# Attention's keys transposed and swapped two slots earlier, and the read-back of results two slots later

## The chip, the cores and the metric

The kernel runs on one core of a Trainium2 chip. The metric is the device time of one execution in microseconds (us). The engines are TensorE (PE), VectorE (DVE), ScalarE (ACT) and GpSimd (POOL); SyncE (SP) issues nearly all DMA transfers of this kernel, in one queue and in the order of the program.

## The reference

Only the first of three stages is touched: attention over 4 batches of 8 heads, 576 positions, 64 columns per head, in float32, with rotated queries and keys.

```python
q_rot, k_rot = (rotate(q), rotate(k))     # x1*cos - x2*sin, x1*sin + x2*cos
scores = scale * np.matmul(q_rot, k_rot.transpose(0, 1, 3, 2))
attn = np.exp(scores - np.max(scores, axis=-1, keepdims=True))
attn = attn / (np.sum(attn, axis=-1, keepdims=True) + 1e-09)
return np.matmul(attn, v)
```

Its result, as a matrix x of 2304 tokens by 512 columns, goes through a gated feed-forward layer (`_moe_ref`) and then through a layer of eight experts, each token to one (`_moe2_ref`).

## The kernel before

**Slots and pairs.** Heads are worked on in 16 pairs, numbered 0 to 15. A pair has nine units of 128 rows of queries, and unit u's scores are made in slot u, so that pair p starts at slot 9p, its base. Slots run from -18 to 152. `step(s)` emits the work of a slot in the order of the string ORDER: exp of the unit before (`soft`), scores, matmuls with the values (`pva`, `pvb`), the copy of their results (`pv_out`), transposes of queries or keys (`qk_T`), the maximum, transposes of the exponentials (`trans`), and `jobs`. No scheduler changes it: each engine takes its instructions in program order.

**Preparation of a pair.** The table AT says how many slots from its base each job of a pair stands. The rotated keys (`rope_a`, `rope_u`, `rope_b` on POOL) are split in a rounded part (`rope_h`, DVE) and a rest (`rope_l`, POOL), both held in the tile `natk`. `qk_T` transposes them on PE in three groups of three, each into the one PSUM bank M of the slot, from which ACT copies them to `Ak`. M and the slot's other uses of it share one tile. `swap` copies `Ak` to `Bk` with its two halves of 64 partitions exchanged, by two DMA transfers, and the scores matmuls read both. Queries go the same way, 10 slots ahead, into `Aq` (tiles `rtq`, `ruq`, `natq`). `Ak` and `Bk` have two buffers each, `rawk` and `rawq` one each, so that the load of the next pair's `rawq` waits for `rope_u` of this pair's queries.

**Results.** A pair's output leaves ACT as two tiles x and goes to the DRAM tensor `xT`, one store (L337) for each of its two heads; the reciprocals of the row sums go to `rT` (L359). For the first two chunks of 384 tokens, eight parts in all, the results are read back while attention still runs: `x_load` (L560, and two or four L569 for the reciprocals) at slot X_FROM + 9i for i from 0 to 7, `x_sum` on POOL three slots later, `x_split` on ACT and DVE seven slots later.

**SP's queue.** Nothing on SP is bound to a slot: a transfer is issued when those before it are and when its own waits are over. Besides its data, each transfer waits for the one eight places before it in the queue.

Of the kernel before, what the change touches and what calls it, by code (L numbers as in the profile page):

```python
# [22 lines left out]
class Attention:  # L23
# [6 lines left out]
    def __init__(self, ctx, tc, q, k, v, tabs, xT, rT, ident):  # L30
# [36 lines left out]
        for p in range(self.NPAIR):  # L67
# [1 line left out]

    AT = {"load k": -22, "load q": -18, "load_v": 1, "rope_a k": -18, "rope_u k": -17, "rope_b k": -16, "rope_h k": -12, "rope_l k": -12, "qk k": (-9, -8, -6),
          "swap": -6, "rope_a q": -10, "rope_u q": -10, "rope_b q": -10, "rope_h q": -8, "rope_l q": -7, "qk q": (-5, -3, -2), "q_pad": 1, "v_split": 5}


    AT_FIRST = ({"rope_a k": -18, "rope_a q": -18, "rope_u k": -17, "rope_b k": -16, "rope_h k": -15, "rope_l k": -15, "qk k": (-14, -13, -12), "rope_u q": -16, "rope_b q": -15, "rope_h q": -14, "rope_l q": -14, "swap": -12, "qk q": (-11, -11, -9), "load_v": -13, "q_pad": 2, "v_split": 6, "load k": -18, "load q": -18},
                {"rope_a k": -18, "rope_u k": -18, "rope_b k": -15, "rope_a q": -16, "rope_u q": -16, "rope_b q": -15, "rope_h k": -10, "rope_l k": -9, "rope_h q": -7, "rope_l q": -4, "qk k": (-6, -5, -3), "swap": -1, "qk q": (-3, -2, 0), "q_pad": 1, "load k": -18, "load q": -18, "v_split": 3, "load_v": -1},
                {"rope_a k": -16, "rope_u k": -16, "rope_b k": -13, "rope_h k": -12, "rope_l k": -10, "load k": -17, "load q": -17, "v_split": 5, "rope_l q": -8, "qk k": (-8, -8, -6), "rope_b q": -8, "rope_a q": -8, "q_pad": 0, "rope_u q": -10})

    def plan(self, p):  # L80
        base = p * self.UNITS
        for what, at in (self.AT | dict(enumerate(self.AT_FIRST)).get(p, {})).items():
            name, *n = what.split()
# [1333 lines left out]
def build(tc, ctx, q, k, v, w_gate, w_val, w_out, w_skip, w_route, w1, w2, cos, sin, tok, cf, out):  # L1417
# [14 lines left out]
    with ExitStack() as part:  # L1432
        at = Attention(part, tc, q, k, v, {"c": cos, "s": sin}, xT, rT, ident)
        for s in at.slots():
# [9 lines left out]
            for lag, fn in ((0, m1.x_load), (X_LAG[0], m1.x_sum), (X_LAG[1], m1.x_split)):  # L1444
                i, rest = divmod(s - lag - X_FROM, at.UNITS)
                if rest == 0 and 0 <= i < 2 * KT:
# [16 lines left out]
EARLY = 4  # L1463
SPLIT_FROM = 6
SPLIT_SLOTS = (3, 7)
X_FROM = 55
X_LAG = (3, 7)

# [26 lines left out]
```

## Time and profile before

| what | value |
|---|---|
| median of 3 runs | 1065.49 us (1062.41 to 1065.62) |
| the profiled execution's own time | 1068.54 us |
| its span, first to last instruction | 1066.7 us |
| PE busy | 984.9 us, 92% |
| ACT, DVE and POOL busy from 0 to 328 us | 247.76, 237.78 and 220.01 us |
| scores matmuls of attention | 14 to 328 us |

The span is the time between the first and the last instruction in the trace; 1.9 us lie around it. Attention takes the first 328 us, and the two other stages follow it.

### The profile page before, as it was taken

What the parts mean: (1) busy time and instruction counts of PE and PEld (TensorE: products, weight loads), DVE (VectorE), ACT (ScalarE), POOL (GpSimd) and SP (SyncE); (2) the same over time, 40 slices, a digit from 0 to 9 for tenths busy, and PEclk for the clock granted to TensorE, in tenths of its full rate; (3) what the DMA queues carried; (4) which work ended last, traced back from release to release, by engine and by line L of the source; (5) the groups of instructions that cost most, each with busy time, mean ns of one, the idle gap of its engine ahead of it and who ended that gap; (6) DMA issues with size and microseconds to landing.
All of it is one profiled execution on the core that took longest, in us unless ns stands there. A gap on an engine that the chain in (4) does not pass through costs nothing. (4 is left out here: it accounts for less than half of the span.)

```text
span 1066.7 us, 16446 instructions
## 1 busy us (share of the span) xinstructions
PE 984.9 (92%) x5893; PEld 816.7 (77%) x5893; DVE 559.4 (52%) x962; ACT 479.5 (45%) x1041; POOL 442.6 (41%) x441
## 2 busy tenths in 40 slices
PE   5999998898899889999999999999999948999896
PEld 4687776676677778789999998999999736786643
DVE  6777777676766888873553342332353314315111
ACT  4888878686776333332441322322344104224122
POOL 6586778677711454553125224124153121112111
PEclk8999999899989999999999999999999968999998
DMA  5345455554423433323320310310421469306191
GB/s 172 88 133 128 131 152 144 147 143 123 127 74 131 122 109 113 104 72 88 100 67 8 95 48 8 96 45 8 133 86 41 135 174 356 103 31 211 30 356 61
DMA packets 81276, 119.80 MB, mean 112 GB/s; under 512 B 36469, under 2 KB 47365, under 8 KB 81168
## 3 DMA queue, kind: packets, MB, share of 16 engines
q1 hardware_dynamic: 77712, 110.01, 34.6%
q0 software_dynamic: 3456, 8.45, 2.6%
q8 instruction: 55, 0.90, 0.4%
q14 instruction: 53, 0.43, 0.1%
HBM read 87.73 MB, written 22.75 MB: 104 GB/s over the span
## 5 line engine op out<-in xcount | busy, mean ns | idle before, releaser
L614 POOL TENSOR_TENSOR hl<-h,hh 128x384 fp32r<-128x384 f32 x72 | 77.9, 1081 | 244.1 <-ACT hh L613 237.9
L251 DVE TENSOR_REDUCE nm<-S 128x1 f32<-128x576 f32 x144 | 108.5, 755 | 46.6 <-PE S L239 45.0
L259 ACT ACTIVATE P<-S,nm 128x576 f32<-128x576 f32 x144 | 107.2, 744 | 4.1 <-DVE nm L251 4.0
L613 ACT CAST hh<-h 128x384 fp32r<-128x384 f32 x72 | 37.0, 514 | 142.7 <-DVE h L612 142.7
L611 DVE TENSOR_TENSOR h<-g,h 128x384 f32<-128x384 f32 x72 | 40.0, 556 | 111.8 <-ACT h L610 111.8
L269 PE MATMUL T<-ident,P 128*128 128x128 f32 x576 | 92.3, 285 | 0.0
L239 PE MATMUL S<-Bk,Aq 128*128 128x288 f32 x256 | 75.6, 309 | 16.2 <-DMA Bk<-Ak 16.2
L627 PE MATMUL Y<-ohi,hl 128*128 128x512 f32 x216 | 85.9, 398 | 1.6 <-POOL hl L614 1.6
L627 PE MATMUL Y<-ohi,hh 128*128 128x512 f32 x216 | 87.1, 403 | 0.0
L318 PE MATMUL pv<-pt,rawv 128*64 128x384 f32 (+1 forms) x512 | 84.8, 433 | 1.5 <-ACT pt L284 1.4
L627 PE MATMUL Y<-olo,hh 128*128 128x512 f32 x216 | 85.3, 395 | 0.0
L239 PE MATMUL S<-Ak,Aq 128*128 128x288 f32 x256 | 83.7, 340 | 1.6 <-ACT P L259 1.6
L604 PE MATMUL g<-xa,ghi 128*128 128x384 f32 x216 | 75.5, 350 | 9.2 <-DVE h L611 8.6
L610 ACT ACTIVATE h<-g 128x384 f32<-128x384 f32 x72 | 35.1, 487 | 87.7 <-PE g L606 83.8
L606 PE MATMUL g<-xa,glo 128*128 128x384 f32 x216 | 72.4, 335 | 0.0
L606 PE MATMUL v<-xa,vlo 128*128 128x384 f32 x216 | 72.2, 334 | 0.0
L604 PE MATMUL v<-xa,vhi 128*128 128x384 f32 x216 | 72.1, 334 | 0.0
L269 PEld LDWEIGHTS T<-ident,P 128*128 128x128 f32 x576 | 65.5, 145 | 2.1 <-issue 1.2
L239 PEld LDWEIGHTS S<-Bk,Aq 128*128 128x128 f32 x256 | 51.5, 201 | 18.5 <-issue 18.1
L612 DVE TENSOR_TENSOR h<-v,h 128x384 f32<-128x384 f32 x72 | 40.2, 558 | 47.7 <-PE v L606 45.3
L239 PEld LDWEIGHTS S<-Ak,Aq 128*128 128x128 f32 x256 | 51.1, 200 | 6.3 <-issue 4.2
L282 DVE COPY pt<-T 128x512 f32<-128x512 f32 x64 | 44.2, 690 | 21.8 <-PE T L269 20.3
(267 smaller groups left out, 2543.6 us busy)
## 6 DMA issues: line engine op xcount, KB each, us to landing
wr_s<-in_moe_w_dram SPq DMA_DIRECT2D x46, 512.0 KB
xT<-x SPq DMA_DIRECT2D x32, 288.0 KB
x<-xT SPq DMA_DIRECT2D x24, 384.0 KB
Bk<-Ak SPq DMA_DIRECT2D x30, 288.0 KB
raw<-in_moe_w_gate_dram SPq DMA_DIRECT2D x12, 512.0 KB
raw<-in_moe_w_val_dram SPq DMA_DIRECT2D x12, 512.0 KB
raw<-in_moe_w_out_dram SPq DMA_DIRECT2D x12, 512.0 KB
wr<-in_moe_w_dram SPq DMA_DIRECT2D x10, 512.0 KB
```

Of the source, the lines that this page charges most:

```text
L239: nc.tensor.matmul(ps[:, c, :288], l, r[:, c * 288:(c + 1) * 288], start=(j == 0), stop=(j == len(ops) - 1))
L251: nc.vector.tensor_reduce(nm, st_u["S"], axis=AX.XY, op=ALU.max, negate=True)
L259: nc.scalar.activation(pt.rearrange("p (a b) -> p a b", a=2), st_u["S"], AF.Exp, bias=st_u["nm"], scale=1.0, accum_out=self.pairs[p]["l"][ ...
L269: nc.tensor.transpose(ps[:, kt * P:(kt + 1) * P], pt[:, kt * P:(kt + 1) * P], self.ident)
L282: self.nc.vector.tensor_copy(self.pt[:, :, cols], self.units[u]["T"])
L318: nc.tensor.matmul(ps[a * D:a * D + D, :n], st["raw"]["v"][:, h, 2 * third + a], self.pt[:, 2 * third + a, c0:c0 + n], start=(third == 0), ...
L604: nc.tensor.matmul(ps[m], wh[:, kt, cols], xh, start=(kt == 0), stop=False)
L606: nc.tensor.matmul(ps[m], wl[:, kt, cols], xh, start=False, stop=(kt == KT - 1))
L611: nc.vector.tensor_tensor(h, ps["g"], h, op=ALU.mult)
L612: nc.vector.tensor_tensor(h, ps["v"], h, op=ALU.mult)
L614: nc.gpsimd.tensor_tensor(hl, h, f32(hh), op=ALU.subtract)
L627: nc.tensor.matmul(self.acc[c][t], a[:, cols], b, start=(f == 0 and i == 0), stop=(f == FT - 1 and i == 2))
```

## The change

Three numbers differ. The three groups of a pair's keys are transposed 11, 9 and 8 slots ahead of its base instead of 9, 8 and 6, and `swap` stands 8 slots ahead instead of 6. Pairs 0 and 1 have values of their own for both and stay as they are. Pair 2 has its own for the transposes and now gets the old one for `swap` too, so that pairs 3 to 15 move. X_FROM is 57 instead of 55, which moves all eight `x_load`, `x_sum` and `x_split` by two slots.

```diff
-    AT = {..., "qk k": (-9, -8, -6),
-          "swap": -6, ...}
+    AT = {..., "qk k": (-11, -9, -8),
+          "swap": -8, ...}
...
-                {..., "qk k": (-8, -8, -6), ..., "rope_u q": -10})
+                {..., "qk k": (-8, -8, -6), ..., "rope_u q": -10, "swap": -6})
...
-X_FROM = 55
+X_FROM = 57
```

**SP's queue**, from the read-back of slot 73 (before) on: `x` and `r` are the read-back, `xT` and `rT` the stores of pair 7, `Bk_9` the swap of pair 9, `rawq_11` the queries of pair 11, `raw_11` weights. Before:

```order
L560 DMA x_0_2_2400<-xT_62 128x2x384
L569 DMA r_0_2_2402<-rT_63 64x384 x2
L337 DMA xT_62<-x_7_0_2338 2x64x576
L359 DMA rT_63<-rr_7_2420 9x128
L206 DMA Bk_9_2462<-Ak_9_2340 64x1152
L207 DMA Bk_9_2462<-Ak_9_2340 64x1152
L104 DMA rawk_11_2521<-in_k_dram 128x576
L337 DMA xT_62<-x_7_1_2448 2x64x576
L457 DMA raw_11_2575<-in_moe_w_val_dram 128x1024
L104 DMA rawq_11_2639<-in_q_dram 128x576
```

Of the change, the same stretch, which like the one before follows the six loads of `rawv_8`:

```order
L206 DMA Bk_9_2390<-Ak_9_2281 64x1152
L207 DMA Bk_9_2390<-Ak_9_2281 64x1152
L337 DMA xT_62<-x_7_0_2335 2x64x576
L359 DMA rT_63<-rr_7_2416 9x128
L560 DMA x_0_2_2457<-xT_62 128x2x384
L569 DMA r_0_2_2459<-rT_63 64x384 x2
L104 DMA rawk_11_2512<-in_k_dram 128x576
L337 DMA xT_62<-x_7_1_2444 2x64x576
L457 DMA raw_11_2573<-in_moe_w_val_dram 128x1024
L104 DMA rawq_11_2634<-in_q_dram 128x576
```

Swap and read-back have changed places: the swap now stands ahead of the store of the first head, and the read-back behind it.

**POOL's queue**, around the sums of the same read-back (`natk_10`, `rtq_10` and `ruq_10` are keys and queries of pair 10, `vt_8` values of pair 8). Before:

```order
L576 TENSOR_TENSOR x_0_2_2400<-x_0_2_2400 128x384
L577 TENSOR_TENSOR x_0_2_2400<-x_0_2_2400,r_0_2_2402 128x384
L221 CAST vt_8_2518<-rawv_8_2385 128x2x64
L222 TENSOR_TENSOR vt_8_2518<-rawv_8_2385,vt_8_2518 128x2x64
L164 TENSOR_TENSOR natk_10_2547<-rtk_10_2356,natk_10_2547 128x9x64
L139 TENSOR_TENSOR rtq_10_2606<-rawq_10_2354,c_115 128x576
L147 TENSOR_TENSOR ruq_10_2608<-rawq_10_2354,s_116 128x9x32 x2
L151 TENSOR_TENSOR rtq_10_2606<-rtq_10_2606,ruq_10_2608 128x576
```

Of the change:

```order
L221 CAST vt_8_2509<-rawv_8_2381 128x2x64
L222 TENSOR_TENSOR vt_8_2509<-rawv_8_2381,vt_8_2509 128x2x64
L164 TENSOR_TENSOR natk_10_2538<-rtk_10_2352,natk_10_2538 128x9x64
L576 TENSOR_TENSOR x_0_2_2457<-x_0_2_2457 128x384
L577 TENSOR_TENSOR x_0_2_2457<-x_0_2_2457,r_0_2_2459 128x384
L139 TENSOR_TENSOR rtq_10_2604<-rawq_10_2350,c_115 128x576
L147 TENSOR_TENSOR ruq_10_2606<-rawq_10_2350,s_116 128x9x32 x2
L151 TENSOR_TENSOR rtq_10_2604<-rtq_10_2604,ruq_10_2606 128x576
```

The two sums of the read-back now stand behind the last step of the keys and directly ahead of the queries.

**PE's queue** in slot 70, the eighth of pair 7 (`S_70` and `S_71` are scores, `M_70` the slot's bank, `T_66` transposed exponentials). Before:

```order
L239 MATMUL S_70_2275<-Bk_7_1901,Aq_7_1922 128x288
L177 MATMUL M_70_2282<-identr_110,natq_8_2118 128x128 x3
L269 MATMUL T_66_2289<-ident_66,P_66_2191 128x128 x4
L239 MATMUL S_71_2298<-Ak_7_1779,Aq_7_1922 128x288
L239 MATMUL S_71_2298<-Bk_7_1901,Aq_7_1922 128x288
```

Of the change:

```order
L239 MATMUL S_70_2269<-Bk_7_1833,Aq_7_1917 128x288
L177 MATMUL M_70_2276<-identr_110,natq_8_2116 128x128 x3
L177 MATMUL M_70_2276<-identr_110,natk_9_2261 128x128 x3
L269 MATMUL T_66_2288<-ident_66,P_66_2185 128x128 x4
L239 MATMUL S_71_2297<-Ak_7_1724,Aq_7_1917 128x288
L239 MATMUL S_71_2297<-Bk_7_1833,Aq_7_1917 128x288
```

Slot 9p + 7 now holds two groups of transposes into one bank, the last one of queries and the first one of the next but one pair's keys.

## Rows read from the trace of the kernel before

**Rows 1.** The page's group of scores matmuls that read Bk; idle before, releaser.

```profile
L239 PE MATMUL S<-Bk,Aq 128*128 128x288 f32 x256 | 75.6, 309 | 16.2 <-DMA Bk<-Ak 16.2
```

**Rows 2.** Busy time by stretch: length, PE, PEld, DVE, ACT, POOL, PEclk, DMA, GB/s.

```profile
53.46:125.75 72.29, 72.29 (x562) 56.08 (x562) 56.84 (x89) 61.30 (x152) 53.75 (x59) 1.00 0.50 131
125.75:143.85 18.10, 18.10 (x142) 14.04 (x141) 14.27 (x23) 15.96 (x39) 16.18 (x18) 1.00 0.55 146
143.85:314.07 170.22, 154.56 (x1121) 118.81 (x1121) 119.14 (x184) 126.04 (x313) 114.52 (x125) 0.94 0.48 130
```

**Rows 3.** Timeline of SP, two rounds and a half: start, length, line, transfer.

```profile
126.07 0.33 SPq L104 DMA_DIRECT2D rawq<-in_q_dram  x1
...
130.31 0.61 SPq L118 DMA_DIRECT2D rawv<-in_v_dram  x1
132.24 0.39 SPq L560 DMA_DIRECT2D x<-xT  x1
...
134.36 0.56 SPq L337 DMA_DIRECT2D xT<-x  x1
...
135.54 0.52 SPq L206 DMA_DIRECT2D Bk<-Ak  x1
136.12 0.59 SPq L207 DMA_DIRECT2D Bk<-Ak  x1
...
194.44 0.38 SPq L560 DMA_DIRECT2D x<-xT  x1
...
201.50 0.54 SPq L337 DMA_DIRECT2D xT<-x  x1
205.68 0.38 SPq L104 DMA_DIRECT2D rawq<-in_q_dram  x1
...
214.29 0.38 SPq L560 DMA_DIRECT2D x<-xT  x1
```

**Rows 4.** SP's own waits to 700 us: total, times, longest.

```profile
SPq L560 <- DMA xT<-x: 10.5, 5, 2.6
```

**Rows 5.** SP's timeline near 318 us; then DMA of 322.8:326.2: packets, MB, share.

```profile
318.12 0.54 SPq L337 DMA_DIRECT2D xT<-x  x1
...
q1 hardware_dynamic: 76, 0.18, 13.0%
```

**Rows 6.** DMA queue of SP in 221:226, then in 226.1:227.8: packets, MB, share.

```profile
q1 hardware_dynamic: 359, 0.98, 80.0%
...
q1 hardware_dynamic: 34, 0.10, 21.9%
```

**Rows 7.** Timeline of POOL: read-back sums and the queries of pair 10.

```profile
198.07 1.01 POOL L576 TENSOR_TENSOR x<-x 128x384 f32<-128x384 f32 x1 [4.34 <-DMA x<-xT]
199.15 1.01 POOL L577 TENSOR_TENSOR x<-x,r 128x384 f32<-128x384 f32 x1
...
202.28 1.87 POOL L139 TENSOR_TENSOR rtq<-rawq,c 128x576 f32<-128x576 f32 x1
204.11 1.54 POOL L147 TENSOR_TENSOR ruq<-rawq,s 128x288 f32<-128x288 f32 x2
205.73 1.59 POOL L151 TENSOR_TENSOR rtq<-rtq,ruq 128x576 f32<-128x576 f32 x1
```

**Rows 8.** Timelines of DVE and PE in the second and fourth slot of pair 6.

```profile
129.11 0.69 DVE L158 CAST natq<-rtq 128x576 fp32r<-128x576 f32 x1
129.72 0.68 DVE L282 COPY pt<-T 128x512 f32<-128x512 f32 x1
...
132.44 0.62 PE L269 MATMUL T<-ident,P 128*128 128x128 f32 x4
```

**Rows 9.** Timelines of PE, ACT and POOL in slot 61, the eighth of pair 6.

```profile
139.80 0.37 PE L177 MATMUL M<-identr,natq 128*128 128x128 f32 x3
...
140.31 0.52 ACT L184 ACTIVATE Aq<-M 128x384 fp32r<-128x384 f32 x1
...
139.35 1.43 POOL L164 TENSOR_TENSOR natk<-rtk,natk 128x576 fp32r<-128x576 f32 x1 [0.40 <-PE T L269]
```

More of the change, by code (lines that the diff above doesn't have):

```diff
@@ L68, in __init__ @@
             self.plan(p)
-    AT = {"load k": -22, "load q": -18, "load_v": 1, "rope_a k": -18, "rope_u k": -17, "rope_b k": -16, "rope_h k": -12, "rope_l k": -12, "qk k": (-9, -8, -6),
-          "swap": -6, "rope_a q": -10, "rope_u q": -10, "rope_b q": -10, "rope_h q": -8, "rope_l q": -7, "qk q": (-5, -3, -2), "q_pad": 1, "v_split": 5}
+    AT = {"load k": -22, "load q": -18, "load_v": 1, "rope_a k": -18, "rope_u k": -17, "rope_b k": -16, "rope_h k": -12, "rope_l k": -12, "qk k": (-11, -9, -8),
+          "swap": -8, "rope_a q": -10, "rope_u q": -10, "rope_b q": -10, "rope_h q": -8, "rope_l q": -7, "qk q": (-5, -3, -2), "q_pad": 1, "v_split": 5}
     AT_FIRST = ({"rope_a k": -18, "rope_a q": -18, "rope_u k": -17, "rope_b k": -16, "rope_h k": -15, "rope_l k": -15, "qk k": (-14, -13, -12), "rope_u q": -16, "rope_b q": -15, "rope_h q": -14, "rope_l q": -14, "swap": -12, "qk q": (-11, -11, -9), "load_v": -13, "q_pad": 2, "v_split": 6, "load k": -18, "load q": -18},
                 {"rope_a k": -18, "rope_u k": -18, "rope_b k": -15, "rope_a q": -16, "rope_u q": -16, "rope_b q": -15, "rope_h k": -10, "rope_l k": -9, "rope_h q": -7, "rope_l q": -4, "qk k": (-6, -5, -3), "swap": -1, "qk q": (-3, -2, 0), "q_pad": 1, "load k": -18, "load q": -18, "v_split": 3, "load_v": -1},
-                {"rope_a k": -16, "rope_u k": -16, "rope_b k": -13, "rope_h k": -12, "rope_l k": -10, "load k": -17, "load q": -17, "v_split": 5, "rope_l q": -8, "qk k": (-8, -8, -6), "rope_b q": -8, "rope_a q": -8, "q_pad": 0, "rope_u q": -10})
+                {"rope_a k": -16, "rope_u k": -16, "rope_b k": -13, "rope_h k": -12, "rope_l k": -10, "load k": -17, "load q": -17, "v_split": 5, "rope_l q": -8, "qk k": (-8, -8, -6), "rope_b q": -8, "rope_a q": -8, "q_pad": 0, "rope_u q": -10, "swap": -6})
     def plan(self, p):
```

## The prediction

> **What bounds the kernel now.** I read the page's groups first: of the scores matmuls' idle time, 16.2 us ends when a swap's transfer to Bk lands [rows 1]. The stretches say where. Pairs 2 to 6 take (72.29 + 18.10) / 5 = 18.08 us each, with PE busy for all of it. Pairs 7 to 14, which run beside the eight read-backs, take 170.22 us, PE is busy for 154.56 of them, and its granted clock averages 0.94 instead of 1.00 [rows 2]. At 18.08 us each they would take 144.6. So these eight pairs lose **25.6 us**, the waits and the slower clock behind them together, and no more can be gained by an earlier swap. Without read-backs the bound is PE, and the swap is just in time.
>
> Next I read SP's timeline. The swap of pair 7 shows why it is late: SP issues six value loads until 130.92, waits for an older store, issues the read-back at 132.24 and a store of results at 134.36, and the swap only at 135.54 [rows 3]. The wait ahead of the read-back is, five times of eight, for a store xT [rows 4].
>
> **What a store does to those behind it.** The last pair's store is issued at 318.12 and still runs in 322.8 to 326.2, alone, with 0.18 MB in these 3.4 us, 53 GB/s, and 13.0% of the 16 engines' time: two engines of the 16 carry it, 26 GB/s each, for 8.1 us from its issue at least [rows 5]. What follows it spreads over all 16. The swap shows the result: until 226 the queue fills 80.0% of the engines, then 21.9% for 1.7 us while its tail follows the store [rows 6]. So a transfer issued behind a store has its last two sixteenths wait for the whole store.
>
> **The change, part by part.**
>
> *The swap.* It now takes the place of the read-back on SP, 3.3 us earlier (132.24 for 135.54), and has no store ahead of it [rows 3]. As its landing was late by a sum of 16.2 us in eight cases, 2.0 us each [rows 1], I cost the swap's own wait at nothing afterwards: -25.6 us.
>
> *The double slot.* The first transposes of keys share bank M with the last ones of queries, and must wait for ACT's copy of these. The query transposes end at 140.17, the copy runs from 140.31 to 140.83 [rows 9]: 0.66 us, and about 0.1 for the two hand-overs, is 0.75. POOL's natk ends at 140.78 and costs nothing more. The work of the transposes itself is only moved. Bounds: 0, if PE had slack there, which a PE busy for 18.10 of 18.10 us excludes [rows 2]; above, 2 us, if ACT, whose copy into Ak must await the next slot's scores, holds up the exponentials queued behind it. ACT has 18.10 - 15.96 = 2.1 us free per pair [rows 2], so I take 0.75. It falls on pairs 2 to 14, 13 times: +9.75 us. A pair without other waits then takes 18.83.
>
> *The read-back.* SP issues it behind the swap and behind the store of the first head, and POOL has its sums directly ahead of the queries. The load of the next rawq waits for `rope_u` of these queries, and everything behind that load on SP, the next swap and read-back too, waits with it. That closes a round:
> - rawq's issue to the swap's: 4.85 us for rawq and the six loads (126.07 to 130.92); with the wait for a store, 8.6 (205.68 to 214.29) [rows 3]. The older store has more time to finish here, so near the lower: 5.5.
> - The swap's issue to the read-back's landing. The two issues take 1.25 with their gap, the store then at least 8.1 [rows 3, 5], and a sixteenth of 384 KB (24.6 KB) at 26 GB/s 0.95: together 10.3 is the lower bound. Above: a store with a swap's tail ahead took 201.50 to 214.25, 12.75 [rows 3], which gives 15.0. Of the swap itself 590 / 16 = 36.9 KB lie ahead on each engine, 1.4 us, and some 0.5 go to the signal: 12.2.
> - The two sums, 198.07 to 200.16, and the queries' first steps, 202.28 to 205.65 [rows 7]: 2.1 + 3.4 = 5.5.
>
> A round takes 23.2 us (bounds 20.7 and 29.1), PE's pair 18.83. What is late next is `rope_h` of the queries on DVE, and behind it the maximum, the exponentials and PE. DVE wants it 3.4 us after the base (125.75 to 129.11), and the copy behind it ends 2.0 us before PE's transposes need its bank (130.40 to 132.44) [rows 8]: 5.4 us of cover. In the first round the read-back lands at 131.0 + 12.2 = 143.2, the sums end at 145.3, the queries at 145.3 + 3.4 + 1.6 = 150.3 [rows 7]; pair 7 starts at 144.6, so that PE needs them by 150.0. The first read-back costs 0.3, the seven others 23.2 - 18.83 = 4.4 each: **+30.9 us**. A clock that falls in these stalls costs nothing more, since the round, not PE, sets the pace then. `x_split` has a slot in which nothing waits for it.
>
> *The rest.* The two later stages keep their program, and only start later or earlier.
>
> **Sum:** -25.6 + 9.75 + 30.9 = **+15.1 us**. On the profiled execution's own time, 1068.54, that is 1083.6; it stands 3.05 us above the median, so a median of **1080.6**.
>
> **A rule of the skill.** Rows 6 show a tail behind a store. The Trainium skill's "DMA: Bandwidth & Descriptors", section "Queues, rings and completion order", says that each engine consumes its descriptors in ring order, and "Why a DMA increments its semaphore by 16 and not by 1" there that a transfer runs on the largest k up to 16 that divides the slowest dimension of both sides, which for the store's 2x64x576 is 2. The trace agrees with both (13.0% of 16 is 2.1 engines). The same page's fit, 2.0 us plus bytes over 436 GB/s, would give the store 2.7 us, and with it the first rival below. It speaks of another path, and the 8.1 us of rows 5 decide.
>
> **The rivals.**
> - *The read-back is not held.* Place: the two engines of the store ahead of L560. If the queue's order didn't bind there, it would land as before, 3.6 us after its issue (194.44 to 198.07) [rows 3, 7], which stands 2.4 us behind the swap's (1.25, and 1.2 for the stores, 134.36 to 135.54); the round takes 5.5 + 6.0 + 5.5 = 17.0, under 18.83, and no query is late. -25.6 + 9.75 = -15.9: **1049.6**, faster. It decides where the round falls under 18.83. For it: the read-back did land so quickly before. Against: it was then issued only after the store had ended [rows 4], and rows 6.
> - *A shorter round.* Near its lower bounds, at 20 us, seven stalls of 1.2: 25.6 less 18.2 is 7.4 gained, **1058**. The result equals before at 25.6 - 9.75 = 15.9 us of stalls, a round of 21.1.
> - *The change doesn't mend the swap, or ACT pays 2 us per double slot.* 13 x 1.25 = 16 us more, with no late query: **1066**, no change. ACT's 2.1 us free [rows 2] speak against.
>
> **How the numbers follow.** Forecast 0.66, read-back not held 0.17, shorter round 0.10, the last 0.07. The forecast alone spans 1069 to 1095, rounds of 21.5 to 25.2. With the second rival the range is 1056 to 1095, and leaves out most of the first and what is over 25.2. A measurement of this kernel tells some 0.3%, 3.2 us, from no change. Faster: 0.17 and 0.08 of the shorter round, 0.25. Same: 0.02 of that, 0.05 of the last, 0.02 of the forecast, 0.09. Slower: 0.66.
>
> **What would show it.** Scores no longer wait for Bk in pairs 7 to 14. PE idles some 0.75 us before the fourth transpose of each slot 9p + 7. POOL still waits for x in each of the eight rounds, and DVE waits 4 to 6 us per round for POOL's rtq, which it didn't before. The rounds from rawq to rawq take 23 us. Wrong I'd be if the read-back lands within 8 us of the swap's issue, if DVE never waits for rtq, or if pairs 2 to 6 lose much more than 0.75 us each.

## The result and the profile after

The changed kernel takes 1080.49 us (median, 1077.65 to 1081.52), the kernel before beside it 1065.55 us: a ratio of 1.0138, with a 95% interval of 1.0105 to 1.0171. It is slower, by 14.9 us. The profiled execution took 1081.52 us, 13.0 us more than the one of before (1068.54).

The page's group of scores matmuls that read Bk, which answers to [rows 1]:

```profile
L239 PE MATMUL S<-Bk,Aq 128*128 128x288 f32 x256 | 72.4, 298 | 1.7 <-DMA Bk<-Ak 1.7
```

The wait for Bk is gone; the 1.7 us belong to pair 1, whose keys and swap the change doesn't touch. The stretches, with the columns of [rows 2]: pairs 2 to 6, then pairs 7 to 14.

```profile
53.97:149.09 95.12, 91.20 (x702) 70.39 (x701) 68.19 (x110) 77.08 (x190) 65.55 (x72) 1.00 0.48 133
149.09:327.15 178.06, 156.81 (x1118) 118.22 (x1118) 125.10 (x185) 124.70 (x313) 119.23 (x128) 0.94 0.44 121
```

A pair without read-backs takes 95.12 / 5 = 19.02 us, where it took 18.08 [rows 2]. The eight pairs with read-backs take 178.06 instead of 170.22. Together with 0.51 us by which pair 2 starts later (53.97 for 53.46), that is 0.51 + 4.73 + 7.84 = 13.1 us, and so all of the loss lies in attention.

The waits of attention (0 to 345 us; total, times, longest):

```profile
POOL x L576 <- DMA x<-xT: 22.3, 7, 4.8
DVE natq L158 <- POOL rtq L151: 16.9, 7, 4.1
PE M L177 <- ACT Aq L184: 10.2, 13, 0.8
```

All three are waits that the prediction named. PE stands 0.78 us in each of 13 double slots. POOL waits for the read-back in seven of eight rounds, and DVE seven times for the queries, which it never did before. A double slot on PE, the last transposes of queries and the first of keys, and then the first and the last of the 13 waits:

```profile
143.84 0.37 PE L177 MATMUL M<-identr,natq 128*128 128x128 f32 x3
145.00 0.43 PE L177 MATMUL M<-identr,natk 128*128 128x128 f32 x3 [0.78 <-ACT Aq L184]
...
49.88 0.43 PE L177 MATMUL M<-identr,natk 128*128 128x128 f32 x3 [0.78 <-ACT Aq L184]
...
298.28 0.43 PE L177 MATMUL M<-identr,natk 128*128 128x128 f32 x3 [0.78 <-ACT Aq L184]
```

Pair 2 starts at 53.97, so the first of these waits lies in pair 1; the last lies in pair 13, whose successor starts at 302.37. The double slots thus stand in pairs 1 to 13, not in 2 to 14 as the prediction has it, because slot 9p + 7 transposes the keys of pair p + 2. Without stalls pairs 7 to 14 would take 7 x 19.02 + 18.1 = 151.2 us, and what a kernel with double slots takes above that is called its stalls here: 178.06 - 151.2 = 26.9 us.

On SP, the start of the first round, the next round from rawq to rawq, and the last such load:

```profile
129.19 0.33 SPq L104 DMA_DIRECT2D rawq<-in_q_dram  x1
...
152.30 0.33 SPq L104 DMA_DIRECT2D rawq<-in_q_dram  x1
...
156.79 0.55 SPq L206 DMA_DIRECT2D Bk<-Ak  x1
...
158.07 0.70 SPq L337 DMA_DIRECT2D xT<-x  x1
...
160.46 0.38 SPq L560 DMA_DIRECT2D x<-xT  x1
...
174.41 0.33 SPq L104 DMA_DIRECT2D rawq<-in_q_dram  x1
...
285.19 0.33 SPq L104 DMA_DIRECT2D rawq<-in_q_dram  x1
```

The same round on POOL:

```profile
169.38 1.01 POOL L576 TENSOR_TENSOR x<-x 128x384 f32<-128x384 f32 x1 [4.14 <-DMA x<-xT]
...
172.82 1.56 POOL L147 TENSOR_TENSOR ruq<-rawq,s 128x288 f32<-128x288 f32 x2
```

And on DVE, the split of the queries that it delays:

```profile
175.91 0.75 DVE L158 CAST natq<-rtq 128x576 fp32r<-128x576 f32 x1 [2.77 <-POOL rtq L151]
```

Read it as a loop. The read-back is issued at 160.46 and POOL gets it at 169.38, 8.9 us later. `rope_u` of the queries ends at 174.38, and 0.03 us later SP issues the next rawq, which waited for that. A round is 22.1 us here, and (285.19 - 152.30) / 6 = 22.15 in the mean, where PE's own pair is 19.02. Only the first, from 129.19 to 152.30, is longer, 23.1 us.

### The profile page after: what moved, and what is told of

The parts are those of the page before. It is cut to its first block, busy times and chain, and to the rows that moved or that the text cites. A ratio compares the mean times of both kernels' runs of the same rounds, so it can differ in the third digit from the quotient of the medians.

```text
span 1079.7 us, 16452 instructions
## 1 busy us (share of the span) xinstructions
PE 985.6 (91%) x5893; PEld 814.4 (75%) x5893; DVE 562.4 (52%) x962; ACT 478.2 (44%) x1041; POOL 443.6 (41%) x441
## 5 line engine op out<-in xcount | busy, mean ns | idle before, releaser
L269 PE MATMUL T<-ident,P 128*128 128x128 f32 x576 | 89.6, 279 | 5.3 <-DVE pt L282 5.2
L239 PE MATMUL S<-Ak,Aq 128*128 128x288 f32 x256 | 81.2, 332 | 1.9 <-ACT P L259 1.9
L239 PE MATMUL S<-Bk,Aq 128*128 128x288 f32 x256 | 72.4, 298 | 1.7 <-DMA Bk<-Ak 1.7
L1190 POOL DMA_INDIRECT out_dram<-o,ix x11 | 11.1, 1007 | 107.5 <-DVE o L1189 75.0
```

Source lines behind the costliest of these rows:

```text
L239: nc.tensor.matmul(ps[:, c, :288], l, r[:, c * 288:(c + 1) * 288], start=(j == 0), stop=(j == len(ops) - 1))
L269: nc.tensor.transpose(ps[:, kt * P:(kt + 1) * P], pt[:, kt * P:(kt + 1) * P], self.ident)
```

## The experiments

"Theory" is the prediction's: two of 16 DMA engines carry a store, the read-back queued behind it is late, and the loop over POOL's queue hands that on to the queries. Of each kernel the stretches of pairs 2 to 6 and of pairs 7 to 14 are compared, with the columns of [rows 2].

**Only the read-back put back.**

```diff
-X_FROM = 57
+X_FROM = 55
```

> The changed kernel with the read-back, its sums and its splits back at slots 55 + 9i. Only that part of the change is undone, keys and swap stay early; SP then issues swap, read-back, store. Theory (the read-back is held by the store ahead of it on the two engines that carry that store): it lands within 4 us of its issue, so a round falls from 22.1 us to about 20, and the eight pairs beside the read-backs stall for some 1 us each instead of 3.2: -25.6 + 13 x 0.95 + 8 x 1.1 = -4, about 1061 us (1056 to 1066). Rival (the cost sits in the earlier keys and swap, wherever the read-back stands): 1076 to 1083 us. POOL's wait for x tells as well: about 1 us or less per round by the theory, where the change has 4.8 at most and 22.3 in all.

Measured: 1067.16 us, ratio to before 1.0022 (1.0002 to 1.0043). The stretch of pairs 7 to 14:

```profile
149.60:314.96 165.36, 149.84 (x1119) 113.96 (x1119) 118.98 (x185) 126.17 (x313) 114.44 (x124) 0.98 0.46 130
```

Two of its waits (0 to 345 us):

```profile
POOL x L576 <- DMA x<-xT: 23.1, 8, 5.9
...
PE M L177 <- POOL natk L164: 15.0, 7, 3.7
```

Its timeline of SP, a rawq with its read-back, and the rawq six rounds later:

```profile
148.53 0.33 SPq L104 DMA_DIRECT2D rawq<-in_q_dram  x1
...
156.73 0.67 SPq L560 DMA_DIRECT2D x<-xT  x1
...
275.35 0.34 SPq L104 DMA_DIRECT2D rawq<-in_q_dram  x1
```

Its timeline of POOL, the first sum of this read-back:

```profile
161.60 1.00 POOL L576 TENSOR_TENSOR x<-x 128x384 f32<-128x384 f32 x1 [4.20 <-DMA x<-xT]
```

The read-back now takes 4.9 us from its issue instead of 8.9, and the stalls fall from 26.9 us to 165.36 - 151.2 = 14.2. So the rival falls. The number was missed by 6 us, though, and lies just above the expected range: the round is (275.35 - 148.53) / 6 = 21.1 us, not 20, and POOL still waits 23.1 us. The sums now stand ahead of natk, and with the keys two slots earlier PE waits for natk 15.0 us, in seven of the 13 double slots. The later read-back had protected the earlier keys from POOL's wait, and cost elsewhere.

**Only the read-back two slots later.** The kernel before, with:

```diff
-X_FROM = 55
+X_FROM = 57
```

> The kernel before with only the read-back two slots later; keys and swap stay as before, so there is no double slot. SP issues store, swap, read-back. Theory: the store's two engines now hold the swap, as before, and the read-back behind it, and POOL's sums stand directly ahead of the queries: the round of some 22 us is there without the earlier swap, pairs 7 to 14 take about 176 us instead of 170.2, pairs 2 to 6 stay at 18.1: about 1071 us (1066 to 1076). Rival (only the double slot and the earlier swap cost time, the later read-back is free): 1066 us or less, and DVE hardly waits for the queries.

Measured: 1070.97 us, ratio 1.006 (1.0037 to 1.0083). Both stretches:

```profile
53.06:143.43 90.37, 90.37 (x701) 70.10 (x701) 71.06 (x111) 77.10 (x191) 64.93 (x72) 1.00 0.51 135
143.43:318.91 175.48, 155.53 (x1122) 119.09 (x1122) 124.10 (x184) 125.94 (x312) 120.96 (x129) 0.94 0.47 125
```

Of its waits:

```profile
DVE natq L158 <- POOL rtq L151: 19.6, 8, 4.1
```

And its page's group of Bk:

```profile
L239 PE MATMUL S<-Bk,Aq 128*128 128x288 f32 x256 | 72.7, 299 | 0.0
```

The pairs with read-backs take 175.5 us, as expected to half a microsecond, and the round is there without the earlier swap. The last row is a trap: the wait for Bk is gone, though the swap's slot is the old one and the slow store still stands ahead of it, and the kernel is slower. The read-back no longer stands ahead of the swap, and pairs of 22 us give it more time; which of the two does it was not tried.

**POOL makes the queries first.** The changed kernel with the sums five slots behind the read-back.

```diff
-X_LAG = (3, 7)
+X_LAG = (5, 8)
```

> The changed kernel with the sums of the read-back five slots behind it instead of three, and the splits eight instead of seven, so that POOL makes the queries first; SP's queue keeps the change's order. Theory (the loop rawq, swap, read-back, sums, queries, rawq sets the pace): the read-back still lands late, but no query waits for it; the loop is open and the eight pairs go at the pace of the others, 19.0 us: -25.6 + 13 x 0.95 = -13, about 1055 us (1050 to 1061). Rival (the late transfers cost PE time by another way than POOL's queries, or POOL's waits for x only move): 1072 to 1082 us.

Measured: 1058.78 us, ratio 0.9953 (0.9939 to 0.9968). Pairs 7 to 14:

```profile
147.28:307.01 159.73, 148.75 (x1118) 113.62 (x1118) 121.42 (x185) 125.75 (x313) 117.41 (x126) 0.99 0.47 134
```

Three of its waits:

```profile
ACT x L333 <- DMA xT<-x: 8.5, 6, 2.5
...
PE pv L318 <- ACT pt L284: 5.8, 4, 2.0
...
POOL x L576 <- DMA x<-xT: 2.6, 3, 1.2
```

The store still stands ahead of the read-back, but no query waits for it, and 18.3 us come back. That is the loop itself, shown open. Of the 26.9 us of stalls 8.5 stay. ACT waits 8.5 us for a tile x whose store hasn't ended, and PE waits 5.8 us for copies pt that ACT makes, a wait that the changed kernel doesn't have; so the slow store seems to reach PE on another way now. That this accounts for all that stays was not tried.

**The store on 16 engines.** The changed kernel, with:

```diff
-            nc.sync.dma_start(self.xT[:, row:row + D, b * S:(b + 1) * S], st["x"])
+            for a in range(2):
+                nc.sync.dma_start(self.xT[a, row:row + D, b * S:(b + 1) * S], st["x"][a * D:(a + 1) * D])
```

> The changed kernel with each store of a head's results made as two transfers of 64 x 576 instead of one of 2 x 64 x 576; the order of everything else is the same, SP has one more issue per head. Theory (the store is slow because two of the 16 engines carry it, and what is queued behind it waits there): spread over 16 engines a store takes less than 3 us, the read-back lands some 4 us after its issue, a round is about 17 us and no query is late: about 1055 us (1050 to 1061). Rival (the order in the queue and the position of the sums cost the time, whatever engines carry the store): 1074 to 1084 us.

Measured: 1055.57 us, ratio 0.9924 (0.9902 to 0.9947). Pairs 7 to 14:

```profile
149.03:304.35 155.32, 147.33 (x1119) 112.63 (x1118) 121.20 (x185) 124.73 (x313) 118.93 (x126) 1.00 0.53 138
```

The transfers of that stretch: count, KB each, median us from issue to landing.

```profile
xT<-x SPq DMA_DIRECT2D x32, 144.0 KB, 2.9
...
x<-xT SPq DMA_DIRECT2D x7, 384.0 KB, 3.5
```

SP's DMA queue from 329.9 to 330.9 us, where two such halves run alone: packets, MB, share of 16 engines.

```profile
q1 hardware_dynamic: 113, 0.22, 101.7%
```

All 16 engines carry the halves, and they move 0.22 MB in 1 us, about 14 GB/s each, where the two engines of a whole store moved 26 each [rows 5]. So the store is about four times as fast, not eight times; what holds the 16 at that rate is not shown. With order and places of the changed kernel, a half lands in 2.9 us, the read-back in 3.5 instead of 8.9, and the stalls are 155.32 - 151.2 = 4.1 us. PE's granted clock is 1.00 in this stretch, where it averaged 0.94 with the stalls.

**Two transfers, but on two engines.** The control: halves by columns, so that the slowest dimension of each stays 2. The changed kernel, with:

```diff
-            nc.sync.dma_start(self.xT[:, row:row + D, b * S:(b + 1) * S], st["x"])
+            for a in range(2):
+                m = S // 2
+                nc.sync.dma_start(self.xT[:, row:row + D, b * S + a * m:b * S + (a + 1) * m], st["x"][:, a * m:(a + 1) * m])
```

> The changed kernel with each store made as two transfers of 2 x 64 x 288, halves by columns, so that there are as many transfers as with the halves by rows, but each still has a slowest dimension of 2. Theory (what counts is that two engines carry the store): nothing is gained, 1078 to 1086 us, and DVE still waits some 17 us for the queries. Rival (two shorter transfers help by themselves, as they are issued and completed apart): 1050 to 1066 us, as with the halves by rows.

Measured: 1087.35 us, ratio 1.0192 (1.017 to 1.0215). Pairs 7 to 14:

```profile
149.28:334.28 185.00, 158.43 (x1119) 118.25 (x1119) 124.90 (x185) 124.54 (x313) 120.97 (x129) 0.94 0.43 119
```

SP's DMA queue from 343 to 346 us, where such halves run alone: packets, MB, share of 16 engines.

```profile
q1 hardware_dynamic: 126, 0.14, 14.0%
```

Its loads of rawq on SP, the first two and the last:

```profile
129.13 1.83 SPq L104 DMA_DIRECT2D rawq<-in_q_dram  x1
...
155.70 0.33 SPq L104 DMA_DIRECT2D rawq<-in_q_dram  x1
...
291.87 0.34 SPq L104 DMA_DIRECT2D rawq<-in_q_dram  x1
```

As many transfers of the same size as with the halves by rows, and nothing is gained: 14.0% of 16 is 2.2 engines, at 0.14 MB in 3 us. What helped was the number of engines, not the second transfer. The time lies 1.4 us above the expected range, and 6.9 us above the changed kernel's by the medians; the intervals of the two ratios just touch at 1.017. In the trace the first round is 26.6 us instead of 23.1, and the six others (291.87 - 155.70) / 6 = 22.7 instead of 22.15. Cut by columns, the packets are half as long as before (0.14 MB in 126 packets, where [rows 5] have 0.18 MB in 76), and the two engines move 47 GB/s instead of 53, a tenth less, where the halves by rows gained a factor of four. Whether that or the second issue makes it slower was not tried.

**The same split in the kernel before.**

```diff
-            nc.sync.dma_start(self.xT[:, row:row + D, b * S:(b + 1) * S], st["x"])
+            for a in range(2):
+                nc.sync.dma_start(self.xT[a, row:row + D, b * S:(b + 1) * S], st["x"][a * D:(a + 1) * D])
```

> The kernel before with each store of a head's results made as two transfers of 64 x 576; nothing else differs. Theory (what made the swap late in the kernel before is the store it follows, on the two engines that carry it): the waits for Bk in pairs 7 to 14 go, without a double slot and without late queries, and the pairs run at 18.1 us: 1065.5 - 25.6 = about 1040 us (1037 to 1046), faster than both kernels. Rival (the swap is late because of its place, two slots too late, whatever the store does): waits for Bk stay above 10 us in sum, 1055 to 1066 us.

Measured: 1042.8 us, ratio 0.9786 (0.977 to 0.9802), faster than both kernels. Both stretches:

```profile
52.27:142.66 90.39, 90.39 (x701) 70.11 (x701) 71.14 (x111) 77.25 (x191) 70.75 (x76) 1.00 0.55 139
142.66:289.47 146.81, 146.26 (x1121) 112.27 (x1121) 119.94 (x184) 125.67 (x313) 115.50 (x125) 1.00 0.56 148
```

The page's group of Bk:

```profile
L239 PE MATMUL S<-Bk,Aq 128*128 128x288 f32 x256 | 72.3, 297 | 0.0
```

The swap at its old place is in time in every pair. Here 23.4 of the 25.6 us that the prediction read from [rows 2] are found, without a double slot.

**The double slot alone.** The kernel before, with:

```diff
-    AT = {..., "qk k": (-9, -8, -6),
+    AT = {..., "qk k": (-11, -9, -8),
```

> The kernel before with only the transposes of the keys two slots earlier; swap and read-back stay. That leaves the double slot alone. Theory (PE waits 0.95 us in each double slot, for ACT's copies): pairs 2 to 6 take 19.03 us instead of 18.08, +4.75; in pairs 7 to 14 the loss lies within the stalls for Bk, which become shorter by as much, so that these stay near 170 us: about 1071 us (1068 to 1074). Rival (it adds to the stalls in every pair): 13 x 0.95 = 12.4 more, about 1078 us.

Measured: 1066.35 us, ratio 1.0012 (0.9993 to 1.0031), under both numbers. Both stretches:

```profile
53.99:149.11 95.12, 91.19 (x702) 70.38 (x701) 68.28 (x110) 77.17 (x191) 70.10 (x76) 1.00 0.51 134
149.11:313.80 164.69, 150.05 (x1118) 114.04 (x1118) 116.60 (x185) 126.22 (x313) 113.46 (x124) 0.98 0.49 130
```

The page's group of Bk:

```profile
L239 PE MATMUL S<-Bk,Aq 128*128 128x288 f32 x256 | 73.9, 303 | 4.6 <-DMA Bk<-Ak 4.6
```

Of its waits:

```profile
PE M L177 <- POOL natk L164: 8.3, 4, 3.3
```

Pairs 2 to 6 lose 4.7 us, exactly as in the whole change. Pairs 7 to 14 gain 5.5, which neither theory expected: the waits for Bk fall from 16.2 to 4.6 us. In part they have only moved: in four of the double slots PE waits for natk, 8.3 us in sum, as with the read-back put back, since POOL's sums stand ahead of natk here too. A pair that is 0.94 us longer also gives the same transfers that much more time; what share of the 5.5 us each has wasn't tried.

**No double slot, split stores.** The changed kernel with the stores split by rows as above, and:

```diff
-    AT = {..., "qk k": (-11, -9, -8),
+    AT = {..., "qk k": (-10, -9, -8),
```

In its new slot the first group takes columns of the bank before two of three small transposes of exponentials are copied from it, so that key values enter these two copies instead; instructions and sizes are the same.

> The changed kernel with the stores in halves by rows and the first group of keys transposed 10 slots ahead instead of 11, so that slot 9p + 7 holds one group only; slot 9p + 8 now holds three small transposes of exponentials and this group in one bank. Theory (the 0.95 us per pair are the wait for ACT's copy of Aq in the double slot): pairs 2 to 6 come back to 18.1 to 18.4 us, and with the stalls of the late queries gone the time is some 1042 to 1047 us. Rival (an earlier swap costs that much wherever the groups stand, as PE or ACT has no room): pairs stay at 19.0 us, about 1055 us.

Measured: 1042.79 us, ratio 0.9791 (0.9774 to 0.9807). Both stretches:

```profile
53.22:143.55 90.33, 90.33 (x702) 70.02 (x701) 69.48 (x111) 77.73 (x193) 68.36 (x74) 1.00 0.54 139
143.55:293.59 150.04, 146.76 (x1119) 112.02 (x1118) 124.27 (x185) 125.02 (x313) 120.17 (x127) 1.00 0.55 144
```

A pair is back at 18.07 us. The 0.94 us are thus the price of awaiting ACT's copy, not of the earlier place, since here nothing awaits a copy. It is no kernel to use, and the one with the old places does as well: with the store repaired, the earlier keys and swap gain nothing, and in the profiled execution pairs 7 to 14 take 150.04 us against 146.81 with the old places.

**The split of the keys a slot earlier.** The changed kernel, with:

```diff
-    AT = {..., "rope_h k": -12, "rope_l k": -12, ...
+    AT = {..., "rope_h k": -13, "rope_l k": -13, ...
```

> The changed kernel with rope_h and rope_l of the keys 13 slots ahead instead of 12, so that POOL's natk is there a slot before the first transposes of keys. Theory (the 0.95 us of a double slot are the waits for ACT's two copies, and natk costs nothing there): pairs 2 to 6 stay at 19.0 us, and the time near 1080 us. Rival (the part of the 0.95 us beyond the 0.78 us of PE's wait for the copy of Aq, 0.17 us, is natk's, whose end the weight load of the transposes awaits): pairs 2 to 6 take about 18.85 us. The whole time tells nothing here, as the rounds set it in the later pairs.

Measured: 1079.62 us in one execution. Pairs 2 to 6:

```profile
53.49:149.36 95.87, 91.64 (x702) 70.47 (x702) 69.63 (x110) 77.07 (x190) 64.23 (x70) 1.00 0.45 129
```

Of its waits:

```profile
PE M L177 <- ACT Aq L184: 10.1, 13, 0.8
```

19.17 us per pair, 0.15 more instead of less, and PE's wait for the copy of Aq is as long as before. So an earlier natk doesn't lower the double slot's price. Why the pair is dearer, in a single execution, was not followed up.

## Why the prediction was right

**The swap's wait, -25.6 us: the mechanism right, the size not measured by itself.** No scores of pairs 2 to 15 wait for Bk any more. But the read-back's rounds now set the pace of these pairs, so that the -25.6 us are only the level from which their stalls are counted; with the store repaired at the old place 23.4 of them were found. Of the "eight cases" the trace has seven in pairs 7 to 14, 15.6 us in sum, and one in pair 1, of 0.6 us, which ends at 34.45; the other 10 us of the loss are PE's longer busy time at the lower granted clock (154.56 - 144.6 [rows 2]). That the store on two engines made the swap late is shown by splitting it at the old place (1042.8 us). The control with two engines (1087.35) was run in the changed kernel only.

**The double slot, +9.75 us: the mechanism right, the size too low.** The term was 0.75 us in 13 pairs. It measured 0.94, or 12.2 us. PE's wait for the copy of Aq is 0.78, as worked out. The rest, 0.16 per pair, is an overlap that the prediction left out. In the kernel before, the matmuls behind the query transposes start ahead of the end of these:

```profile
140.01 0.63 PE L269 MATMUL T<-ident,P 128*128 128x128 f32 x4
```

The transposes end at 140.17 [rows 9], 0.16 us later. The prediction counted the wait from that end, as the profile does, but what PE loses counts from 140.01. In the double slot shown above, the next matmul starts 145.00 - 143.84 = 1.16 us after the query transposes' start, where it was 0.21: 0.95 more. In the stretches the 0.16 us stand as busy time, 91.20 us in pairs 2 to 6 where there were 90.39 [rows 2]. That natk costs nothing there agrees with the last experiment. ACT does wait 1.5 us in each double slot for the next slot's scores, the prediction's upper bound, but in pairs 2 to 6 that doesn't reach PE.

**The read-back, +30.9 us: the mechanism right, the size too high.** Stalls are 26.9 us. The round's three parts, by the rows above, against the prediction's:

| part | predicted | measured |
|---|---|---|
| rawq's issue to the swap's | 5.5 | 4.5 |
| swap's issue to the read-back's landing | 12.2 | 12.6 |
| sums, and queries up to `rope_u` | 5.5 | 5.0 |
| round | 23.2 | 22.1 |

The first part was taken near its lower bound of 4.85 and lies below it: SP met no wait for a store there, and the loads themselves were issued some 0.5 us quicker than in the round of [rows 3]. Pair 7, pairs 8 to 13 and pair 14 of the change, with the columns of [rows 2]:

```profile
149.09:169.48 20.39, 18.55 (x141) 14.10 (x141) 16.18 (x25) 15.51 (x40) 13.64 (x16) 1.00 0.49 133
169.48:302.37 132.89, 117.62 (x841) 88.67 (x841) 94.39 (x139) 93.47 (x234) 95.07 (x99) 0.95 0.46 128
302.37:327.15 24.78, 20.64 (x138) 15.46 (x138) 14.53 (x23) 15.73 (x40) 10.53 (x14) 0.86 0.27 69
```

Pairs 8 to 13 stall (132.89 - 6 x 19.02) / 6 = 3.1 us each, just what the round gives (22.15 - 19.02), instead of 4.4. The first read-back, which I had let off for 0.3, costs 20.39 - 19.02 = 1.4. The last pair stalls 24.78 - 18.1 = 6.7: DVE's longest wait, 4.1 us, falls there, and PE is busy 20.64 us at a granted clock of 0.86. So that a slower clock costs nothing in the stalls, as the prediction has it, holds where a round follows, but in the last pair it has some 2.5 us of the 6.7. DVE's wait per round, a sign that the prediction put at 4 to 6 us, is 16.9 / 7 = 2.4, at most 4.1.

**The sum.** -25.6 + 12.2 + 26.9 = +13.5, where the profiled executions differ by 13.0; most of the rest is pair 1, in which 0.51 of the 0.94 us show. +15.1 was predicted. One term 2.5 too low and one 4.0 too high partly cancel, and the profiled executions stand 3.0 and 1.0 us above their medians. That the median of 1080.49 meets the forecast of 1080.6 so closely is in part chance. Nor do the two parts of the change add up: the later read-back alone has a ratio of 1.006, the earlier keys and swap alone 1.0022, and both together 1.0138.

**The rivals.** "The read-back is not held" fell: it landed 12.6 us behind the swap's issue, where that rival needed 6. With the store on 16 engines its mechanism is what happens, but at 1055.6 us, not 1049.6, because of the dearer double slot and 4.1 us of stalls. "A shorter round" needed 21.1 us or less to come out even; the round was 1 us over that. "The change doesn't mend the swap, or ACT pays 2 us per double slot" fell with the group of Bk and with the 0.94 us.

**The rule of the skill.** The Trainium skill's "DMA: Bandwidth & Descriptors", section "Why a DMA increments its semaphore by 16 and not by 1", takes the largest k up to 16 that divides the slowest dimension of both sides: 2 for the store, 16 for a half by rows, 2 for a half by columns. The runs agree with all three: 13.0% of 16 is 2.1 engines for the store [rows 5], 101.7% is all 16 for the halves by rows, and 14.0% is 2.2 for the halves by columns. The same page of the Trainium skill gives a fit for another path, by which I weighed the first rival. For a half of 147 KB it would give 2.3 us, as an estimate; the trace has 2.9. For the whole store it would give 2.7 us, and the trace has 8.1 at least [rows 5].

## What to carry to other kernels

When a transfer is late, look first at what stands ahead of it in the queue and over how many engines that is spread; a slow store repaired in place gave 22 us, and moving others out of its way lost 15. Follow a moved step through every in-order queue that it passes, and look for a loop: a load that waits for an engine that waits for a transfer behind that load sets a pace of its own, and its length against the bound engine's is the number to work out. A wait that disappears from the profile is no proof of a repair, as it may have been covered by a longer one.

## What the hardware showed that I had not expected

All 16 engines, busy throughout, move the halves by rows at some 14 GB/s each, where two engines alone moved a whole store at 26 each. Cut by columns instead, the same store gains nothing: with packets half as long, the two engines move 47 GB/s instead of 53. And a wait that the profile gives as 0.78 us starts PE's next matmul 0.95 us later, at a granted clock of 1.00, because the profile counts the wait from the end of the last matmul, where otherwise the next one would have started 0.16 us ahead of that end.
